# A gather issued one expert earlier, and a routing step moved behind value products, in a fused retention, mixture-of-experts and attention kernel

## The chip, the cores and the metric

The kernel runs on one core of a Trainium2 chip. The metric is the device time of one execution in microseconds (us); lower is better. Engines are named as the profile names them: PE (TensorE; PEld are its weight loads), DVE (VectorE), ACT (ScalarE), POOL (GpSimd) and SP (SyncE, which issues most transfers). Each engine does its instructions in the order in which the program gives them to it.

## The reference

Three layers follow one another, for 2 sequences of 768 tokens, in float32.

```python
# 1. retention: 8 heads of 64, gamma of each head fixed
for t in range(S):
    state = gamma * state + outer(k[:, :, t], v[:, :, t])
    y[:, :, t] = scale * (q[:, :, t] @ state)
x = y as rows of 512

# 2. one expert of 8 for each token; a gate lets a token keep the expert of the token before it
for s in range(S):
    fresh_e = argmax(logits[b, s])                 # logits = x @ w_gate
    e = fresh_e if s == 0 or local_gate[b, s] < 0.5 else prev_e
    prev_e = e
    p = softmax(logits[b, s])
    out[b, s] = p[e] * (relu(x[b, s] @ w1[e]) @ w2[e])     # 512 -> 1024 -> 512

# 3. four causal attention heads of 64; each token takes the two best of them, weighted
for e in range(E2):
    ye = softmax(causal(scale * q_e @ k_e.T)) @ v_e @ wo[e]
    out += weight_of_head(e) * ye
```

## The kernel before, in words

Stage 1 does the retention in six chunks of 128 tokens, for both sequences (0 and 1) in each. For chunk c it has the scores (L307, made at the end of the chunk ahead), which DVE fades with the decay (`fade`, L311, two instructions for each sequence), the products of the past (`outputs_past`, L340), the value products (`outputs_now`, L349, 16 for each sequence), the evacuation of the output by ACT (`evacuate`, L354), and the update of the state (L363, L372). POOL multiplies the decay into keys and queries of the next chunk (`decay_k`, L331; `decay_q`, L325). Q, k and v come in halves of a block, 512 KB each, two chunks ahead.

Between these steps stands the routing of the chunk ahead (class `Route`). `turn_pair` brings the output into rows and the logits beside them (L383, L386). `first` marks the fresh expert (L450 to L461, with a product L453 and its evacuation L458); `held` multiplies the marks `fo` by an identity (PE, L464) and scans along the tokens (DVE, L467), so that a kept token gets the expert of the token before it; `count` scans again (L471) for the place of each token in its expert. Later come `offset`, `rank`, `columns`, `slots`, `marks` (L496), `tokens` (L502, it writes `tt`), `hots` (L507) and `table` (L513), which makes the lists of the tokens of each expert. `shares` (L439, L441) makes the softmax with `nm`, the negated maximum, on DVE and exponentials on ACT. The products L453, L464 and `columns` write parts of one PSUM tile, pR, and `marks` and `tokens` read it. In chunks 4 and 5 some of the first expert's weight pieces are split into a high part `whi` (ACT, L186) and a low part `wlo` (DVE, L191). `busy` (L229) issues dense matmuls on a tile of zeros, whose results nobody reads.

Stage 2 goes over the experts in order of size. Expert e has a hidden half (L873, or L885 and L887) and a value half (`second`, L914 and L918), both on weight pieces that are split five pieces ahead (`prepare`). Its token rows are gathered from x1_d by two indirect DMAs, which POOL issues (`gather`, L220); `gather(e, None)` only reserves the two tiles of a ring of four. `turn2` transposes the gathered rows of expert e + 1 on PE (L809) within the value half of expert e. At the end `put(0)` and `put(1)` scatter the two halves of the result into x2_d, by indirect DMAs that POOL issues too (L940).

Stage 3 does the attention on the rows of x2_d.

In all of stages 1 and 2 the order on every engine is the order of the program text (`manual_schedule`). The order of the parts in a chunk c of stage 1 is:

```python
pYs = [outputs_past(n) for n in ns]
...                                   # columns, slots, first, table, marks, tokens
RT[c - 1].held()                      # PE L464, DVE L467
RT[c - 1].count()                     # DVE L471
RT[c - 2].hots(0, B)                  # DVE L507
for n, pY in zip(ns, pYs):
    outputs_now(n, pY, 0, H // 2)     # PE L349
    evacuate(n, pY)                   # ACT L354
```

Of the kernel before, what the change touches and what calls it, by code (L numbers as in the profile page):

```python
# [21 lines left out]
B, H, S, D = 2, 8, 768, 64  # L22
DM = H * D
C = 128
NC = S // C
# [83 lines left out]
def kernel(  # L109
# [25 lines left out]
    GI = cst.tile([128, 2, E], I32, name="GI")  # L135
# [47 lines left out]
    def split_high(i):  # L183
        hi = ring.tile([128, 1024], F32R, name="whi", bufs=PIECES)
        lo = ring.tile([128, 1024], F32R, name="wlo", bufs=PIECES)
        nc.scalar.activation(hi, raws[i], AF.Copy)  # L186
        pieces[i] = (hi, lo)
# [25 lines left out]
    def gather(e, ix):  # L213
        if e >= E:
            return
        for i in range(2):
            if ix is None:
                XG[e, i] = ring.tile([128, RW], F32, name="xg", bufs=4)
                continue
            nc.gpsimd.indirect_dma_start(  # L220
                out=XG[e, i], out_offset=None, in_=x1_d[:, :],
                in_offset=bass.IndirectOffsetOnAxis(ap=ix[:, i, e:e + 1], axis=0), bounds_check=T, oob_is_err=False)
# [4 lines left out]
    def busy(pw, n, w=4):  # L227
        for _ in range(n):
            nc.tensor.matmul(pw[:, :w * 128], WZ, WZ[:, None, :].to_broadcast([128, w, 128]), start=True, stop=True)  # L229
# [7 lines left out]
    def bank(kind, shape):  # L237
        return psum[-1].tile(shape, F32, name=kind, bufs=2 if kind == "A" else 3)

    with tc.tile_pool(name="s1", bufs=2) as s1:  # L240
        XB, QT, KD, QD, AM, XR, XT, LL = {}, {}, {}, {}, {}, {}, {}, {}
# [8 lines left out]
        def load_pair(c, x):  # L250
            if c >= NC:
                return
            for b in range(B):
                load_half(c * B + b, x)
# [28 lines left out]
        pB = bank("B", [128, 512])  # L283
# [15 lines left out]
        def scores(n, kind):  # L299
            c, b = divmod(n, B)  # L300
            x = XB[n, 0]
            AM[n] = s1.tile([128, 2, H // 2, C], F32, name="am")
            PA[n] = [bank(kind, [128, H // 2, C]) for _ in range(2)]
            for a in range(H // 2):
                for j in range(2):
                    r = slice(j * D, (j + 1) * D)
                    nc.tensor.matmul(PA[n][j][:, a, :], x[r, 1, a * 128:(a + 1) * 128],  # L307
                                     x[r, 0, a * 128:(a + 1) * 128], start=True, stop=True)

        def fade(n, j):  # L310
            nc.vector.tensor_tensor(out=AM[n][:, j], in0=PA[n][j], in1=DT[:, j], op=OP.mult)  # L311
# [15 lines left out]
        def decay_k(n):  # L327
            c, b = divmod(n, B)
            if c < NC - 1:
                KD[n] = s1.tile([128, H, D], F32, name="kd")  # L330
                nc.gpsimd.tensor_tensor(out=KD[n], in0=XB[n, 1][:, 0].rearrange("p (h d) -> p h d", h=H),  # L331
                                        in1=cn("ktab").rearrange("p (c h) -> p c h", c=NC)[:, c, :, None]
                                        .to_broadcast([128, H, D]), op=OP.mult)
# [10 lines left out]
        def outputs_now(n, pY, a0, a1):  # L344
            x = XB[n, 1]
            for a in range(a0, a1):
                for j in range(2):
                    h = 2 * a + j
                    nc.tensor.matmul(pY[j * D:(j + 1) * D, a, :], x[:, 1, h * D:(h + 1) * D], AM[n][:, j, a, :],  # L349
                                     start=n < B, stop=True, skip_group_check=True)  # L350

        def evacuate(n, pY):
            XT[n] = s1.tile([128, H // 2, C], F32, name="xT")
            nc.scalar.activation(XT[n], pY, AF.Copy)  # L354
# [62 lines left out]
        rows, RT = {}, {}  # L417
# [106 lines left out]
        with tc.manual_schedule(engines={ENG.PE, ENG.DVE, ENG.Activation, ENG.Pool, ENG.SP}):  # L524
            for b in range(B):
                decay_k(b)
                scores(b, "AC"[b])
                busy(pB, 3 - b)
                for j in range(2):
                    fade(b, j)  # L530
            nc.gpsimd.tensor_copy(IB, ident)
# [4 lines left out]
            for c in range(NC - 1):  # L536
                load_pair(c + 2, 0)
                if c >= 2:
                    RT[c - 2].offset()
                    RT[c - 2].rank()  # L540
                if c >= NC - 3:
                    fetch_piece(3 * (c - NC + 3))
                if c:
                    part, logits, pv = turn_pair(c - 1)
                    l2 = s1.tile([128, B, E + 1], F32, name="l2")
                    part(0, 8)
                    for b in range(B):
                        logits(b, l2)
                    put_rows(pv)
                    for b in range(B):  # L550
                        send_rows(B * (c - 1) + b)
                if c == 2:
                    nc.sync.dma_start(x1_d[0:1, :], ZR[0:1])
                    for b in range(B):
                        t = b * S + (NC - 1) * C + 1
                        nc.sync.dma_start(x1_d[t:t + C, :], ZR)
                ns = [B * c + b for b in range(B)]
                pYs = [outputs_past(n) for n in ns]
                if c >= 2:
                    RT[c - 2].columns()  # L560
                    RT[c - 2].slots(0, B)
                if c:
                    RT[c - 1] = Route(c - 1)
                    RT[c - 1].first(LL[c - 1], 0, B)
                if c >= 3:
                    RT[c - 3].table(0, B)
                if c >= 2:
                    RT[c - 2].marks(0, B)
                    RT[c - 2].tokens(0, B)
                if c:  # L570
                    RT[c - 1].held()
                    if c == NC - 2:
                        split_high(0)
                    RT[c - 1].count()
                if c >= 2:
                    RT[c - 2].hots(0, B)
                for n, pY in zip(ns, pYs):
                    outputs_now(n, pY, 0, H // 2)
                    evacuate(n, pY)
                    if c == NC - 2 and n == ns[0]:  # L580
                        split_high(1)
                for n in ns:
                    state(n)
                for n in ns:
                    keep(n)
                load_pair(c + 2, 1)
                if c == 1:
                    nc.gpsimd.memset(ZR, 0.0)
                if c >= NC - 3:
                    for i in ((1, 2), (4,))[c - NC + 3]:  # L590
                        fetch_piece(i)
                if c:
                    RT[c - 1].shares(LL[c - 1], 0, B)
                next_qt(c + 2)
                nn = [B * c + 2 + b for b in range(B)]
                if c == NC - 2:
                    split_low(0)
                    split_low(1)
                    nc.gpsimd.tensor_copy(TF[:, :1], pieces[1][1][:, :1].bitcast(F32))
                for f in (decay_k, decay_q)[::1 if c else -1]:  # L600
                    for n in nn:
                        f(n)
                for n in nn:
                    scores(n, "AC"[n % 2])
                    for j in range(2):
                        fade(n, j)
            c = NC - 1
# [19 lines left out]
            V = RT[c - 1] = Route(c - 1)  # L627
# [3 lines left out]
            X.table(0, B)  # L631
            W.marks(0, B)
            W.tokens(0, B)
            V.held()
            V.shares(LL[c - 1], 0, B)
            V.count()
            W.hots(0, B)
            U = Route(c)
            xs = [s1.tile([128, B, DM], F32R, name="blq", bufs=4) for _ in range(2)]
# [34 lines left out]
                                     start=False, stop=m == 1 and b == 1, skip_group_check=True)  # L674

            outputs_now(n0, pYs[0], 0, H // 2)
            evacuate(n0, pYs[0])
            outputs_now(n1, pYs[1], 0, H // 2)
            evacuate(n1, pYs[1])
# [60 lines left out]
            for x in range(2):  # L740
                n = slice(2 * x, 2 * x + 2)
# [55 lines left out]
    with tc.tile_pool(name="mx", bufs=2) as mp:  # L797
# [42 lines left out]
        order = ExitStack()  # L840
        order.enter_context(tc.manual_schedule(engines={ENG.PE, ENG.DVE, ENG.Activation, ENG.Pool, ENG.SP}))
        for e in range(E):
            gather(e + 1, None)
            gather(e + 1, GI)
            if e == 0:
                gather_shares(GS)
            if e == E - 1:
# [9 lines left out]
            def hide():  # L857
                for hi, lo, src in later:
                    nc.scalar.activation(hi, src, AF.Relu)  # L859
                    nc.vector.scalar_tensor_tensor(lo, src, 0.0, hi.bitcast(F32), op0=OP.max, op1=OP.subtract)  # L860
                later.clear()

            for f in range(4):
# [4 lines left out]
                if N > JOIN:  # L868
                    ph = bank("B", [128, 2, CAP])
                    for a in range(2):  # L870
                        n = slice(a * 128, (a + 1) * 128)
# [6 lines left out]
                else:  # L878
                    hc = hh[:, :, 128:] if N <= 192 else None
                    hs.append((hh, hl, hc))  # L880
                    for a in range(2):
                        n = slice(a * 128, (a + 1) * 128)
# [14 lines left out]
                        later.extend(parts)  # L897
                prepare(8 * e + f)
            hide()
            pys = []  # L900
            for i in range(2):
                pys.append(bank("C", [128, DM]))
# [51 lines left out]
            else:  # L954
# [40 lines left out]
                for x in range(2):  # L995
                    n = slice(2 * x, 2 * x + 2)
# [452 lines left out]
```

## Time and profile before

| | |
|---|---|
| time, median of 3 runs | 398.82 us (397.45 to 399.89) |
| the profiled execution: time, span | 398.97 us, 397.2 us |
| stage 1, by the start of its last parts | 0 to about 74 us |
| stage 2 | about 74 to 255 us |
| stage 3 | about 255 to 397 us |
| PE busy | 381.2 us, 96% of the span |
| DVE, ACT, POOL busy | 277.7 us, 237.0 us, 121.2 us |
| mean granted clock of PE | 0.992 |

A row of the timeline has a start, a length, the engine, a line of the kernel, an operation and what it writes and reads, and how many equal instructions were merged into it. In brackets stands how long the engine was idle before it, and what ended that wait. Such a releaser is inferred from semaphores; where an instruction waits for several, the last by the profile is named, and where that one had long been done it was another, often a DMA. Matmuls are pipelined, and their ends are modelled.

### The profile page before, as it was taken

The numbers are of one execution on the slowest core, as the hardware profiler recorded it, in microseconds if no ns is written. First come the engines' busy times: TensorE is split into PE (matmuls) and PEld (weight loads), VectorE is DVE, ScalarE is ACT, GpSimd is POOL, SyncE is SP. The second block draws the span as 40 slices with busy tenths as digits, with TensorE's granted clock in tenths as the row PEclk, the third lists the DMA queues.
The fourth block names the chain that finished last, engine by engine and source line by source line (L and its number), as shares of the span: only waits on it lengthen the run. The fifth ranks groups of instructions, "written<-read, shape, count | busy, mean of one in ns | idle before, by whom it ended". The sixth has DMA issues, their size and how long they took to land.

```text
span 397.2 us, 8425 instructions
## 1 busy us (share of the span) xinstructions
PE 381.2 (96%) x2960; PEld 332.8 (84%) x2960; DVE 277.7 (70%) x785; ACT 237.0 (60%) x547; POOL 121.2 (31%) x175
## 2 busy tenths in 40 slices
PE   8999999999999999989899999999999999999993
PEld 3889996998979797878788698899889988988772
DVE  4556696885676868687787983278986887779630
ACT  1566674283555756677777872267775765668751
POOL 3744432221305012131213020435545332415520
PEclk9999998999999999999999999999999999999998
DMA  7998967477675767777777862131011001001011
GB/s 244 398 358 290 339 234 259 138 252 229 222 248 183 228 231 252 250 227 227 241 242 243 291 235 69 68 115 54 5 50 53 29 2 54 2 27 52 31 54 60
DMA packets 23609, 67.38 MB, mean 170 GB/s; under 512 B 4469, under 2 KB 4725, under 8 KB 23560
## 3 DMA queue, kind: packets, MB, share of 16 engines
q1 hardware_dynamic: 21010, 59.35, 44.7%
q0 software_dynamic: 2544, 7.42, 5.6%
q8 instruction: 25, 0.41, 0.4%
q14 instruction: 24, 0.20, 0.2%
q10 hardware_dynamic: 6, 0.01, 0.0%
HBM read 56.17 MB, written 11.07 MB: 169 GB/s over the span
## 4 chain that ended last, share of the span: by engine, by line
PE 82%; DVE 7%; DMA 5%; ACT 4%; issue 1%; POOL 0%; SPq 0%; POOLq 0%; DVEq 0%; ACTq 0%
PE C L918 18%; PE B L873 8%; PE C L1062 8%; PE C L1238 5%; PE B L1218 5%; PE A L1168 5%; PE C L1257 4%; PE C L1099 4%; DMA xg<-x_d,GI 3%; PE C L349 3%; DVE wlo L191 2%; PE A L307 2%; ACT whi L186 2%; PE A L809 2%; PE A L383 1%; PE B L885 1%
## 5 line engine op out<-in xcount | busy, mean ns | idle before, releaser
L191 DVE TENSOR_TENSOR wlo<-wraw,whi 128x1024 fp32r<-128x1024 f32 x64 | 77.0, 1223 | 16.0 <-ACT whi L186 15.3
L186 ACT ACTIVATE whi<-wraw 128x1024 fp32r<-128x1024 f32 x64 | 65.6, 1049 | 1.3 <-DMA wraw<-in_w_dram 1.2
L940 POOL DMA_INDIRECT x_d<-y,SI x16 | 18.4, 1149 | 136.8 <-ACT y L930 96.0
L1199 POOL TENSOR_SCALAR a<-a,mx,wt 128x128 f32<-128x128 f32 (+5 forms) x48 | 34.2, 721 | 50.4 <-DVE mx L1195 12.8
L918 PE MATMUL C<-whi,hh 128*128 128x512 f32 (+4 forms) x112 | 45.5, 406 | 0.0
L1189 ACT ACTIVATE a<-a,mx 128x128 f32<-128x128 f32 (+5 forms) x48 | 32.0, 668 | 21.5 <-DVE mx L1180 18.3
L918 PE MATMUL C<-whi,hl 128*128 128x512 f32 (+4 forms) x112 | 44.2, 394 | 0.0
L918 PE MATMUL C<-wlo,hh 128*128 128x512 f32 (+4 forms) x112 | 44.1, 394 | 0.0
L885 PE MATMUL B<-xx,whi 128*128 128x384 f32 (+3 forms) x100 | 30.9, 363 | 0.0
L1180 DVE CUSTOM_DVE_ANT_0 a<-A,MR 128x384 f32<-128x384 f32 (+3 forms) x48 | 25.3, 530 | 2.4 <-PE A L1168 2.0
L1218 PE MATMUL B<-K,a 128*128 128x128 f32 x168 | 26.3, 274 | 0.0
L887 PE MATMUL B<-xx,wlo 128*128 128x192 f32 (+3 forms) x100 | 25.7, 257 | 0.0
L918 PEld LDWEIGHTS C<-whi,hl 128*128 128x128 f32 (+4 forms) x112 | 20.0, 179 | 5.9
L918 PEld LDWEIGHTS C<-wlo,hh 128*128 128x128 f32 (+4 forms) x112 | 20.1, 180 | 4.9
L918 PEld LDWEIGHTS C<-whi,hh 128*128 128x128 f32 (+4 forms) x112 | 20.1, 179 | 4.5
L859 ACT ACTIVATE hh<-t 128x128 fp32r<-128x128 f32 (+4 forms) x56 | 16.3, 318 | 12.1 <-DVE t L891 9.9
L1218 PEld LDWEIGHTS B<-K,a 128*128 128x128 f32 x168 | 19.8, 140 | 2.4 <-issue 0.7
L1168 PE MATMUL A<-ks,qh 128*128 128x256 f32 (+3 forms) x56 | 21.6, 385 | 0.1
L1238 PE MATMUL C<-at,vv 128*64 128x256 f32 (+1 forms) x192 | 21.5, 359 | 0.0
L220 POOL DMA_INDIRECT xg<-x_d,GI x14 | 15.6, 1116 | 13.2 <-DVE z L763 9.2
L1238 PEld LDWEIGHTS C<-at,vv 128*64 128x64 f32 x192 | 13.4, 136 | 7.2 <-issue 1.4
L885 PEld LDWEIGHTS B<-xx,whi 128*128 128x128 f32 x100 | 18.8, 188 | 0.6
(321 smaller groups left out, 980.6 us busy)
## 6 DMA issues: line engine op xcount, KB each, us to landing
wraw<-in_w_dram SPq DMA_DIRECT2D x64, 512.0 KB, 4.2
blq<-in_blk_dram SPq DMA_DIRECT2D x12, 512.0 KB, 7.9
blk<-in_blk_dram SPq DMA_DIRECT2D x12, 512.0 KB, 6.6
x_d<-xr SPq DMA_DIRECT2D x12, 260.0 KB, 7.5
out_dram<-y SPq DMA_DIRECT2D x12, 256.0 KB, 2.0
xr<-x_d SPq DMA_DIRECT2D x10, 256.0 KB, 2.6
x_d<-ZR SPq DMA_DIRECT2D x2, 260.0 KB, 5.9
wraw<-in_wv_dram SPq DMA_DIRECT2D x1, 520.0 KB
```

Source lines behind the costliest of these rows:

```text
L186: nc.scalar.activation(hi, raws[i], AF.Copy)
L191: nc.vector.tensor_tensor(out=lo, in0=raws.pop(i), in1=hi.bitcast(F32), op=OP.subtract)
L873: nc.tensor.matmul(ph[:, a, :N], w[:, k, n], x[:, k, :N], start=m == 0, stop=m == 11)
L885: nc.tensor.matmul(pa[:, :, :N], wh[:, k, n], XX[e][:, k, :, :N], start=k == 0, stop=False, skip_group_check=True)
L887: nc.tensor.matmul(pa[:, 1, :N], wl[:, k, n], XX[e][:, k, 0, :N], start=False, stop=k == 3, skip_group_check=True)
L918: nc.tensor.matmul(pys[i][:rows], h[:, a, n], w[:, a, :], start=f == 0 and a == 0 and m == 0, stop=f == 3 and a == 1 and m == 2)
L1062: nc.tensor.matmul(pp, w[:, k, a * 128:(a + 1) * 128], x[:, k, :], start=m == 0, stop=m == 11)
L1168: nc.tensor.matmul(ps[:, :w], qq[b, g, e][:, tq], KS[b, e][:, s0:s0 + w], start=m == 0, stop=m == 1)
L1189: nc.scalar.activation(AA[u][:, :n], AA[u][:, :n], AF.Exp, bias=mx[:, 0, i:i + 1], scale=-1.0, accum_out=mx[:, 1, i:i + 1])
L1199: nc.gpsimd.tensor_scalar(a[:, :n], a[:, :n], mx[:, 1, i:i + 1], WT[b, g][:, i, e:e + 1], op0=OP.mult, op1=OP.mult)
L1218: nc.tensor.transpose(pT[:, s - s0, :], a[:, s * C:(s + 1) * C], ident)
L1238: nc.tensor.matmul(po[j * HD:(j + 1) * HD, c0:], VV[b, s][:, e * HD:(e + 1) * HD], at[j][:, s, c0:], start=s == 0, stop=s == ns - 1, skip_ ...
```

## The change

Three things change, in order of place.

First, the dense matmuls between the scores of chunk 0 become fewer: 1 instead of 3 behind the scores of sequence 0, none instead of 2 behind those of sequence 1.

Second, `held` and `count` of the chunk ahead move, in each of the chunks 1 to 5, from before the value products to behind those of the first sequence and before their evacuation. In chunk 5 `shares` moves with them. In chunk 4 the split of weight piece 0 on ACT, which stands between the two, goes along.

Third, in stage 2 the gather for expert e + 2 is issued between the hidden half and the value half of expert e, from e = 1 on. The gathers for experts 1 and 2 stay at the start of experts 0 and 1. Until now the gather for e + 1 was issued at the start of e.

```diff
@@ -525,7 +525,7 @@
                 scores(b, "AC"[b])
-                busy(pB, 3 - b)
+                busy(pB, 1 - b)
                 for j in range(2):
                     fade(b, j)
@@ -567,15 +567,15 @@
                     RT[c - 2].marks(0, B)
                     RT[c - 2].tokens(0, B)
-                if c:
-                    RT[c - 1].held()
-                    if c == NC - 2:
-                        split_high(0)
-                    RT[c - 1].count()
                 if c >= 2:
                     RT[c - 2].hots(0, B)
                 for n, pY in zip(ns, pYs):
                     outputs_now(n, pY, 0, H // 2)
+                    if c and n == ns[0]:
+                        RT[c - 1].held()
+                        if c == NC - 2:
+                            split_high(0)
+                        RT[c - 1].count()
                     evacuate(n, pY)
                     if c == NC - 2 and n == ns[0]:
                         split_high(1)
@@ -631,9 +631,6 @@
             W.marks(0, B)
             W.tokens(0, B)
-            V.held()
-            V.shares(LL[c - 1], 0, B)
-            V.count()
             W.hots(0, B)
@@ -674,6 +671,9 @@
             outputs_now(n0, pYs[0], 0, H // 2)
+            V.held()
+            V.shares(LL[c - 1], 0, B)
+            V.count()
             evacuate(n0, pYs[0])
             outputs_now(n1, pYs[1], 0, H // 2)
             evacuate(n1, pYs[1])
@@ -840,8 +840,9 @@
         for e in range(E):
-            gather(e + 1, None)
-            gather(e + 1, GI)
+            if e < 2:
+                gather(e + 1, None)
+                gather(e + 1, GI)
             if e == 0:
                 gather_shares(GS)
@@ -897,6 +898,9 @@
                 prepare(8 * e + f)
             hide()
+            if e:
+                gather(e + 2, None)
+                gather(e + 2, GI)
             pys = []
```

## Rows read from the trace of the kernel before

**Rows 1.** The page: span, and busy time of PE (share, instructions).

```profile
span 397.2 us, 8425 instructions
...
PE 381.2 (96%) x2960; PEld 332.8 (84%) x2960; DVE 277.7 (70%) x785; ACT 237.0 (60%) x547; POOL 121.2 (31%) x175
```

**Rows 2.** Waits of PE, 0 to 75 us: for whom, us, times, longest.

```profile
PE B L464 <- DVE tt L502: 2.3, 4, 0.7
...
PE B L464 <- DVE fo L461: 0.7, 1, 0.7
```

**Rows 3.** Waits of PE, 75 to 260 us.

```profile
PE A L809 <- DMA xg<-x_d,GI: 3.1, 3, 1.5
PE A L809 <- DVE hh L860: 1.2, 1, 1.2
```

**Rows 4.** Timeline around expert 3: start, length, instruction, idle before and releaser.

```profile
141.58 1.03 POOL L940 DMA_INDIRECT x_d<-y,SI  x1 [12.44 <-ACT y L930]
...
148.41 0.93 POOL L940 DMA_INDIRECT x_d<-y,SI  x1 [5.79 <-DVE hl L860]
149.65 1.40 POOL L220 DMA_INDIRECT xg<-x_d,GI  x1 [0.30 <-issue]
...
154.91 0.63 PE L809 MATMUL A<-K,xg 128*128 128x128 f32 x4 [0.55 <-DMA xg<-x_d,GI]
```

**Rows 5.** Timeline of PE, the first transposes within expert 5.

```profile
197.58 0.63 PE L809 MATMUL A<-K,xg 128*128 128x128 f32 x4 [1.25 <-DVE hh L860]
```

**Rows 6.** Timeline of PE, the held product of chunk 2.

```profile
30.32 0.23 PE L464 MATMUL B<-IB,fo 128*128 128x128 bf16 x1 [0.68 <-DVE tt L502]
```

**Rows 7.** Timeline of chunk 0: scores, dense matmuls, fades, value products.

```profile
6.67 1.93 PE L307 MATMUL A<-blq 64*128 64x128 f32 x16 [0.16 <-DMA blq<-in_blk_dram]
...
8.52 0.82 PE L229 MATMUL B<-WZ 128*128 128x512 bf16 x3
8.62 1.29 DVE L311 TENSOR_TENSOR am<-A,DT 128x512 f32<-128x512 f32 x2 [2.16 <-PE A L307]
...
9.28 1.16 PE L307 MATMUL C<-blq 64*128 64x128 f32 x16
...
10.37 0.60 PE L229 MATMUL B<-WZ 128*128 128x512 bf16 x2
...
10.90 1.99 PE L349 MATMUL C<-am,blk 128*64 128x128 f32 x32
```

**Rows 8.** Timeline of chunk 1: POOL's decays, DVE's first comparison, value products.

```profile
14.80 2.52 POOL L325 TENSOR_TENSOR qd<-blq,qt 128x512 f32<-128x512 f32 x2 [1.91 <-DMA qt<-in_qtab_dram]
...
17.28 2.04 POOL L331 TENSOR_TENSOR kd<-blk,K 128x512 f32<-128x512 f32 x2
...
18.41 0.94 DVE L450 TENSOR_TENSOR eq<-L,K 128x16 bf16<-128x16 f32 x1
...
20.55 1.97 PE L349 MATMUL C<-am,blk 128*64 128x128 f32 x32
```

**Rows 9.** Windows: stretch, length, busy PE, PEld, DVE, ACT, POOL, granted clock, DMA, GB/s.

```profile
20.50:30.40 9.90, 9.22 (x136) 8.83 (x135) 5.74 (x19) 5.99 (x18) 4.51 (x4) 1.00 0.99 345
50.30:60.40 10.10, 9.44 (x144) 9.07 (x143) 9.36 (x24) 7.04 (x17) 3.96 (x5) 1.00 0.58 219
206.00:228.70 22.70, 21.22 (x120) 17.64 (x119) 18.53 (x34) 17.49 (x31) 4.56 (x4) 1.00 0.79 263
```

**Rows 10.** Timeline of chunks 4 and 5: first fades, tokens, `nm`, first evacuation.

```profile
54.36 1.29 DVE L311 TENSOR_TENSOR am<-A,DT 128x512 f32<-128x512 f32 x2
...
60.02 0.18 DVE L502 TENSOR_TENSOR tt<-B,K 128x32 bf16<-128x32 f32 x1
...
60.93 0.14 DVE L439 TENSOR_SCALAR nm<-mx 128x2 f32<-128x2 f32 x1
...
61.69 0.57 ACT L354 ACTIVATE xT<-C 128x512 f32<-128x512 f32 x1
```

**Rows 11.** Windows of half a us, the tail of stage 1, with the granted clock.

```profile
66.50:67.00 0.50, 0.50 (x3) 0.23 (x2) 0.47 (x2) 0.50 (x2) 0.25 (x1) 0.50 0.12 49
```

## Prediction

> **What bounds the kernel now.** I read the page first, then the busy time by stretch, then the waits of TensorE (PE), then the timeline around each wait. The page says that PE is busy 381.2 us of the 397.2 us of the span [rows 1]. So the kernel is bound by PE, and whatever a reordering can win lies in the 16 us in which PE stands still. The waits of PE name two places that the diff touches. In stage 1 the held product (L464) waits five times, 0.7 + 2.3 = 3.0 us in all, for VectorE (DVE) to finish `fo` or `tt` [rows 2]. PE works in order, so the 32 value products of the chunk (L349), which need neither, stand behind it. In stage 2 the transposes of the next expert's rows (L809) wait four times, 3.1 us by name for the gathered rows and 1.2 us by name for DVE [rows 3]. These are the prices on offer, 7.3 us; the question is how much of each arrives at the end.
>
> **The gather, place and price.** Look at expert 3 in the order of GpSimd (POOL) [rows 4]. The first scatter of the expert ahead is issued at 141.58. The second is issued only at 148.41, 6.8 us later. The view names a DVE instruction for this wait, but both scatters write x2_d, and 6.8 us is what one needs to land: I read it as the landing of the first scatter. The gather comes behind the second scatter in POOL's order and is issued at 149.65. PE gets to the transposes and waits 0.55 us, until 154.91, 5.3 us after the issue. The gather is thus late because POOL's queue holds it behind two scatters that follow one another.
>
> The edit puts the gather for expert e + 2 between the hidden half and the value half of expert e. On POOL nothing but the gathers stands between the second scatter of e - 1 and the first scatter of e, and a gather waits for no result of the hidden half. So it will be issued where today's gather for e + 1 is issued, just behind the second scatter of e - 1; what changes is that these rows are wanted one whole expert later. Its buffer is free: the ring has four, and the rows of expert e, which lie in the same two, were transposed in the value half of e - 1. Each gather is two DMAs on POOL's queue, as before, and their number is the same; only during expert 1 are there four in a row (for 2, then for 3). The two for 2 are first, so nothing that is wanted soon stands behind the new ones. POOL's next work, the first scatter of e, has to wait for the whole value half anyway.
>
> I count the fourth wait (197.58, 1.25 us [rows 5], put down to DVE `hh`) as a gather's too: the products of the value half ahead of it in PE's queue have used those `hh` already. Price: 3.1 + 1.2 = 4.3 us. If that fourth wait were DVE's own, 3.1. What cover takes over? Behind the transposes PE needs the weight pieces; nothing in the waits of stage 2 is put down to them today [rows 3], so I take no new wait, and keep the weights as a rival.
>
> **Held product and count, chunks 1 to 3.** The edit moves L464 behind the first 16 value products, 0.9 us by the starts of L349. `tt` is ready by then in chunk 2, where L464 stood idle 0.68 us [rows 6], and the scan behind it on DVE comes 0.3 us later than today while `hots` is done in its place: no loss there, since DVE next waits for scores. Chunk 2 gives 0.68; the other three waits on `tt` share 2.3 - 0.68 = 1.6, some 0.54 each, so chunk 3 gives 0.54. Together 1.2 us.
>
> Chunk 1 is different, and the warm-up is part of it. The edit takes four of the five dense matmuls (L229) out of chunk 0. They lie on PE's path: three take 0.82 us, and the second scores follow them [rows 7]. With one left, the second scores begin 0.55 earlier, at 8.75, and end at 9.9. The first pair of fades also ends at 9.91 (8.62 + 1.29), so the first value products start there. The second fades then run from 9.95 to 11.25; today's second value products start at about 11.8 (10.90 + 0.9). So chunk 0 gains about 0.5 us, not 4 x 0.27 = 1.1. Of this, little passes through chunk 1. There DVE's first comparison (L450) takes 0.94 us and ends at 19.35, just as POOL's pair of decay products ends (17.28 + 2.04 = 19.32) [rows 8]. That pair follows the `qd` pair, which began at 14.80, when the DMA of `qt` landed. A transfer's landing does not move with PE. I take L450's end as fixed at 19.35; a product with its result stands ahead of the value products, so these start at about 19.5 instead of 20.55: 1.05 us from chunks 0 and 1 together. Were L450 simply long, it would move along and the sum would be 0.5 + 0.7 = 1.2; the bounds lie close.
>
> The Trainium skill (GPSIMD Engine Reference, section Specifications) says that POOL shares its SBUF interfaces with DVE and contends with DVE instructions that read two SBUF inputs. L450 is such an instruction, and by that rule its end stays with POOL's: 1.05, not 1.2.
>
> **Chunks 4 and 5.** Here DVE is the engine to watch: it is busy 9.36 of 10.1 us [rows 9]. In chunk 4 it has the split of two weight pieces between `count` and the fades, and runs without a pause to the fades at 54.36 [rows 10]. Reordering saves it only the 0.1 us by which its wait for L464 gets shorter (0.33 today, some 0.2 behind `hots`). The same holds in chunk 5, where `tt` ends at 60.2 behind a third split. And there `shares` moves as well: its `nm` (60.93) releases two exponentials on ScalarE (ACT) that stand ahead of the evacuation of the first output (61.69) in ACT's order, after the edit as now. `nm` comes behind `hots` and the scan, which is 0.1 earlier at best. So of the 1.1 us of PE waits in these two chunks I take 0.15 us; the bounds are 0 and 1.1. The rest of stage 1 (60 to 74) is a chain of short steps and moves along.
>
> **Sum.** Stage 1: 1.05 + 1.2 + 0.15 = 2.4. Stage 2: 4.3. Together 6.7 us. Stage 3 is not touched. The profiled execution took 398.97 us (span 397.2), 0.15 above the median of 398.82, so the two need no correction: 398.97 - 6.7 = 392.3 us.
>
> **Rivals.**
> A, the forecast, 392.3. Its own range comes from the bounds: the fourth wait DVE's own (1.2 less) to chunks 4 and 5 given whole (0.95 more) and chunk 1 at 1.2: 391.1 to 393.5.
>
> B, the transfers hold stage 1. In its chunks the DMA engines are busy 0.99 of the time [rows 9], and a shorter chunk wants the same bytes sooner. Against it: PE waits for a chunk's load only at the very start (the first scores), and the loads are two chunks ahead. If nothing of stage 1 comes, 398.97 - 4.3 = 394.7.
>
> C, the weights take the place of the gather. In expert 6 the DMA engines are at 0.79, and DVE is busy 18.5 of 22.7 us [rows 9]; take the stall away and DVE is at 18.5 of 21.2. A value product would then wait for `wlo`. Against it: splits run five pieces ahead, and no wait of PE is put down to them. Half of stage 2's gain lost gives 394.5, all of it 396.6; I take 395.5.
>
> D, slower: the clock. By its durations PE began at its lower level: the 16 products of the first scores started over 1.85 us (6.67 to 8.52), those of the next over 1.09 (9.28 to 10.37), 1.7 times as fast [rows 7]. The four dense matmuls came just behind that rise, and in a sparse stretch of the tail the granted clock does fall, to 0.50, the 1.2 GHz level [rows 11]. If the clock fell back after the edit, each us of full-speed work would take 0.7 us more. 6.7 / 0.7 = 9.6 us of such work use up the whole gain, 15 us make the kernel over 1% slower; two chunks (18 us of PE work) would give 392.3 + 12.6 = 405. Against it: the clock had already risen before the matmuls that go, and the later chunks, which hold no dense matmul and stood idle at the held product, kept 1.00 [rows 9].
> The Trainium skill (TensorE: Matmul & The Clock Gate, Part 1) says that the throttled clock is the default and that activity releases it. By that rule fewer warm-up matmuls can only hurt; that is D. The rows agree that PE starts low.
>
> That the edit of the gather does nothing, because POOL waits in between, is no rival of weight: its index and buffers are ready.
>
> **How the numbers follow.** A 0.63, B 0.14, C 0.15, D 0.04; 0.04 is left for what I do not see. The likeliest gives 392.3. The range reaches below A for runs that lie as far from the median as those of before (397.45 to 399.89) and above to B and most of C: 390.6 to 395.2. One per cent, about what a measurement of this kernel tells from no change, is 4.0 us, so faster means below 394.8. A lies there, B at its edge (half), C by a third: 0.63 + 0.07 + 0.05, and 0.02 of the unseen: 0.77. D and a little of the unseen are slower: 0.05. The rest, 0.18, is the same.
>
> **What would show it.** Right: no wait of L464 in chunks 2 and 3, none of L809; the gather for e + 2 issued just behind the second scatter of e - 1; L450 of chunk 1 still ending at about 19.35; `nm` of chunk 5 later behind its `tt` than today. Wrong: idle time of L349, L307 or the decay products put down to a load (B); of L918 to `wlo` (C); 16 scores over 1.8 us after the first ones (D); L809 still waiting at expert 5 (the fourth wait was DVE's).

## The result, and the profile after

| | before | changed kernel |
|---|---|---|
| time, median of 11 runs | 399.32 us (397.45 to 400.49) | 394.23 us (391.96 to 397.19) |
| ratio to before | | 0.9886, 95% interval 0.9853 to 0.9918 |
| the profiled execution: time, span | 398.97, 397.2 us | 394.20, 392.4 us |
| PE busy | 381.2 us | 381.4 us |

The kernel became faster by 1.1%, 4.6 us by the ratio; the forecast was 6.7 us and 392.3. The span of the profiled execution became 4.8 us shorter, all of it idle time of PE. These are the waits of PE in the changed kernel, up to 72 us and from 72 to 256 us; they answer to [rows 2] and [rows 3].

```profile
PE B L229 <- DVE WZ L231: 1.0, 1, 1.0
PE A L645 <- ACT xT L354: 0.6, 1, 0.6
PE B L874 <- ACT x0h L725: 0.2, 1, 0.2
...
PE B L963 <- DMA xg<-x_d: 1.4, 1, 1.4
PE B L874 <- ACT x0h L725: 0.2, 1, 0.2
```

No wait of the held product (L464) and none of the transposes (L809) is left. Three waits are new: 0.6 us before the gate products in the tail of stage 1 (L645, L648 before), 0.2 us in the first products of stage 2 (L874, L873 before; it lies at 72 us and so stands in both answers), and 1.4 us before the first rows within expert 7 (L963, L959 before). The starts of PE's parts, read from both timelines, show where the time came from and where it went:

| stretch of PE, from and to the start of | before | after | difference |
|---|---|---|---|
| span's start, first scores | 6.67 | 6.44 | -0.23 |
| first scores, value products of chunk 1 | 13.88 | 12.82 | -1.06 |
| chunk 1 to chunk 2 | 9.93 | 9.33 | -0.60 |
| chunk 2 to chunk 3 | 9.93 | 9.52 | -0.41 |
| chunks 3 to 5 | 20.01 | 19.03 | -0.98 |
| chunk 5, stage 2 | 13.20 | 14.17 | +0.97 |
| stage 2, value half of expert 7 | 166.29 | 161.68 | -4.61 |
| value half of expert 7, first rows | 5.58 | 7.16 | +1.58 |
| first rows, end of the span | 151.71 | 152.25 | +0.54 |

The differences add up to -4.8. At the value half of expert 7 the changed kernel was 6.9 us ahead.

**The gather.** The timeline around expert 3 (compare [rows 4]):

```profile
146.21 1.05 POOL L944 DMA_INDIRECT x_d<-y,SI  x1 [5.50 <-DVE t L892]
147.56 1.58 POOL L220 DMA_INDIRECT xg<-x_d,GI  x1 [0.30 <-PE B L888]
...
152.29 0.60 PE L809 MATMUL A<-K,xg 128*128 128x128 f32 x4
```

The gather (now of expert 5) is issued right behind the second scatter, as before. The transposes at 152.29 (of expert 4's rows, gathered an expert earlier) have no idle time ahead of them.

**The new wait within expert 7.** Timeline of the changed kernel from the last splits of expert 6 to the first rows:

```profile
221.67 1.06 ACT L186 ACTIVATE whi<-wraw 128x1024 fp32r<-128x1024 f32 x1 [1.32 <-DMA wraw<-in_w_dram]
...
223.30 1.06 ACT L186 ACTIVATE whi<-wraw 128x1024 fp32r<-128x1024 f32 x1 [0.57 <-DMA wraw<-in_w_dram]
...
224.78 1.06 ACT L186 ACTIVATE whi<-wraw 128x1024 fp32r<-128x1024 f32 x1 [0.42 <-DMA wraw<-in_w_dram]
...
225.75 0.67 ACT L934 ACTIVATE y<-C,pc 128x512 f32<-128x512 f32 x1
...
226.69 1.27 POOL L944 DMA_INDIRECT x_d<-y,SI  x1 [18.01 <-ACT y L934]
...
232.01 3.52 POOL L944 DMA_INDIRECT x_d<-y,SI  x1 [4.04 <-DVE hl L876]
...
234.62 0.68 DVE L876 SCALAR_TENSOR_TENSOR hl<-B,hh 128x512 fp32r<-128x512 f32 x1
...
237.39 0.80 SPq L853 DMA_DIRECT2D xg<-x_d  x2
...
240.15 1.24 PE L963 MATMUL B<-K,xg 128*128 128x128 f32 x8 [1.42 <-DMA xg<-x_d]
```

And the same steps before:

```profile
229.08 1.06 ACT L186 ACTIVATE whi<-wraw 128x1024 fp32r<-128x1024 f32 x1 [0.47 <-DMA wraw<-in_w_dram]
...
230.05 0.67 ACT L930 ACTIVATE y<-C,pc 128x512 f32<-128x512 f32 x1
230.99 1.33 POOL L940 DMA_INDIRECT x_d<-y,SI  x1 [13.24 <-ACT y L930]
...
236.69 1.44 POOL L940 DMA_INDIRECT x_d<-y,SI  x1 [4.37 <-DVE hl L875]
...
240.14 0.80 SPq L852 DMA_DIRECT2D xg<-x_d  x2
...
245.49 1.03 PE L959 MATMUL B<-K,xg 128*128 128x128 f32 x8
```

Read these rows against the start of expert 7's hidden half (228.51 before, 221.59 after). PE reached the first rows 17.0 us behind it before, and would have after. ACT stands 2.3 us on weight pieces that have not landed (1.2 us before): its last split came 4.3 us earlier than before (229.08, 224.78), for a PE that was 6.9 us ahead. The evacuation stands behind that split and came 1.5 us behind the start of the hidden half before and 4.2 us after. Its result goes into the first scatter, the second scatter waits for the first one (it began 8.2 us behind that start before, 10.4 us after), and the load of the first rows waits for both.

This lateness is only half of it. The second scatter also took 3.52 us on POOL instead of 1.44; it lies beside DVE instructions that follow one another without a pause, and it ended 0.23 us behind the last of them (`hl` at 234.62). So the load was issued 15.8 us behind that start instead of 11.6. Before, by an estimate with the 2.76 us from the load's issue to the first rows after (237.39 to 240.15), it had 2.6 us to spare. The lateness of the second scatter (2.2 us) or its length (2.1 us) alone would have fitted into that; the two together did not.

### The profile page after: what moved, and what is told of

Its sections match the earlier page's. It is cut to its first block, busy times and chain, and to the rows that moved or that the text cites. A ratio compares the mean times of both kernels' runs of the same rounds, so it can differ in the third digit from the quotient of the medians.

```text
span 392.4 us, 8418 instructions
## 1 busy us (share of the span) xinstructions
PE 381.4 (97%) x2956; PEld 333.8 (85%) x2956; DVE 275.5 (70%) x785; ACT 235.5 (60%) x547; POOL 124.9 (32%) x175
## 4 chain that ended last, share of the span: by engine, by line
PE 75%; DVE 10%; ACT 8%; issue 3%; DMA 3%; ACTq 0%; SPq 0%; DVEq 0%
PE C L922 13%; PE C L1066 7%; PE B L874 6%; ACT whi L186 5%; PE C L1242 5%; PE B L1222 5%; PE C L1261 4%; PE A L1172 4%; PE C L1103 4%; DVE wlo L191 4%; PE C L349 3%; PE B L886 2%; PE C L340 2%; PE B L229 2%; PE A L307 2%
## 5 line engine op out<-in xcount | busy, mean ns | idle before, releaser
L944 POOL DMA_INDIRECT x_d<-y,SI x16 | 21.1, 1318 | 128.0 <-ACT y L934 86.2
## 6 DMA issues: line engine op xcount, KB each, us to landing
blk<-in_blk_dram SPq DMA_DIRECT2D x12, 512.0 KB, 10.2
```

## The experiments

The kernels e1 to e12 stand below in the order e1, e2, e3, e4, e5, e10, e6, e7, e12, e9, e8, e11.

**Each part alone.** Four kernels hold one part or two. In the first only the gather moved:

```diff
 # before, with
+            if e < 2:
-            gather(e + 1, None); gather(e + 1, GI)
+                gather(e + 1, None); gather(e + 1, GI)
...
             hide()
+            if e:
+                gather(e + 2, None); gather(e + 2, GI)
```

> Of the change only the gather for expert e + 2 in the middle of expert e; stage 1 is that of the kernel before. The forecast's sum: the four waits of L809 go, 4.3 us, and nothing takes their place: about 395.0 (before at 399.3). Rival, from the profile of the changed kernel: with stage 2 shorter the last weight pieces come late, ScalarE waits for them with the evacuation of expert 6's first half behind it, and so the scatter and the load of the first rows (L959) come late: PE waits there for 1 to 1.5 us, and the gain is about 3 us, 396.3. The wait of L959 on the load tells the two apart.

Measured: 394.61 us, ratio 0.9881 (0.985 to 0.9911). The gather alone brings as much as the whole change. From stage 2's start to expert 7's value half its profile has 161.27 us against 166.29, 5.0 us less. Then comes the rival's wait:

```profile
PE B L963 <- DMA xg<-x_d: 2.4, 1, 2.4
```

So both are right in part. The forecast's time (395.0) was met by the median, and the gain of stage 2 is larger than forecast, but a loss stands behind it. In the profiled execution (395.14) the two together leave 2.4 us, not 4.3. The rest of its 3.8 us of shorter span comes mainly from stretches that this edit does not touch: the first scores begin 0.6 us earlier, the stretch from them to chunk 1 is 0.3 us shorter, and that from chunk 5 to stage 2 is 0.5 us shorter.

In the second only `held`, `count` and `shares` moved:

```diff
 # before, with
-                if c:
-                    RT[c - 1].held()
...
                     outputs_now(n, pY, 0, H // 2)
+                    if c and n == ns[0]:
+                        RT[c - 1].held()
...
-            V.held(); V.shares(LL[c - 1], 0, B); V.count()
...
             outputs_now(n0, pYs[0], 0, H // 2)
+            V.held(); V.shares(LL[c - 1], 0, B); V.count()
```

> Of the change only held, count and shares behind the first value products; all five dense matmuls stay and the gathers stay where they were. Forecast: chunk 1 gives its wait, 0.7 us, chunks 2 and 3 together 1.2, chunks 4 and 5 with the tail 0.15: 2.0 us, about 397.3. If shares did not stand ahead of the evacuation the last two chunks would give another 1.0: 396.3.

Measured: 397.40 us, ratio 0.9964 (0.9938 to 0.9991): 1.4 us, with 2.0 (a ratio of 0.995) inside the interval and 3.0 outside. No wait of L464 is left in its profile, and the 0.6 us before the gate products is there.

In the third only the warm-up shrank:

```diff
-                busy(pB, 3 - b)
+                busy(pB, 1 - b)
```

> Of the change only one dense matmul instead of five in chunk 0. Forecast's step: chunk 0 gains 0.5 us; L450 of chunk 1 ends at 19.35 as now, tied to GpSimd, PE waits for it, and 0.1 to 0.4 us arrive at the end: about 399.0. Rival: L450 moves along, and 0.5 us arrive. Rival (clock): with fewer dense matmuls the granted clock stays at 1.2 GHz for longer, at the start or in the tail of stage 1, in some executions: mean granted clock under 0.990 and 1 to 3 us longer.

Measured: 398.44 us, ratio 0.9987 (0.9968 to 1.0006). L450 of chunk 1 did not end at 19.35 in its profile but at 18.78, and PE did not wait for it. The time lies between no change and 1.3 us; 0.1 to 0.4 fits, and the full 1.1 us cannot be told apart from it by this alone. Ten of its 12 executions had a mean granted clock of 0.995 or more: the fewer dense matmuls did not keep the clock low.

The fourth is the changed kernel with the line above put back.

> The changed kernel with all five dense matmuls back in chunk 0. By the forecast 0.3 to 0.6 us slower than the changed kernel: 394.5 to 394.8. Rival (clock): the executions of the changed kernel differ by 5 us and those with a mean granted clock of 0.988 are the longer ones; if the missing matmuls cause that, these executions stay at 0.993 and about 393, as fast as the changed kernel or faster.

Measured: 393.80 us, ratio 0.9881 (0.9846 to 0.9915), the same as the changed kernel; the 0.3 to 0.6 us of the expectation are too small to be seen here. Two of its six executions had a mean clock of 0.988 and took 396.4 and 396.8, so the missing matmuls are not what makes such executions. Its profile is one of them. The windows of one us around the first rows (columns as in [rows 9]):

```profile
240.00:241.00 1.00, 0.00 (x0) 0.00 (x0) 0.66 (x2) 0.30 (x1) 0.00 (x0) 1.00 0.88 303
241.00:242.00 1.00, 0.62 (x5) 0.50 (x6) 0.21 (x1) 0.69 (x1) 0.00 (x0) 0.96 0.37 139
242.00:243.00 1.00, 1.00 (x6) 1.00 (x6) 0.00 (x0) 0.00 (x0) 0.33 (x1) 0.50 0.00 0
243.00:244.00 1.00, 1.00 (x4) 0.81 (x3) 0.00 (x0) 0.00 (x0) 0.69 (x1) 0.50 0.00 0
244.00:245.00 1.00, 1.00 (x4) 0.71 (x4) 0.00 (x0) 0.00 (x0) 0.00 (x0) 0.50 0.69 262
245.00:246.00 1.00, 1.00 (x5) 0.83 (x4) 0.00 (x0) 0.00 (x0) 0.00 (x0) 0.83 0.00 0
246.00:247.00 1.00, 1.00 (x6) 0.79 (x5) 0.00 (x0) 0.00 (x0) 0.00 (x0) 1.00 0.00 0
```

PE stands 2.0 us in front of the first rows, and then the granted clock is 0.50, the 1.2 GHz level, for over 3 us of dense work. From the first rows to stage 3 this execution took 10.83 us instead of 9.09: the wait is paid a second time, with 1.7 us.

**The wait within expert 7.** Evacuation and scatters of expert 6 go ahead of the last splits:

```diff
                     second(f, 1)
+                    if e == E - 2 and f == 3:
+                        put(0)
+                        put(1)
                     prepare(8 * e + 4 + f)
...
-                put(0)
-                put(1)
+                if e < E - 2:
+                    put(0)
+                    put(1)
```

> The changed kernel, in which expert 6 evacuates and scatters its result before the last weight splits of its value half, not behind them. Theory: these splits wait on ScalarE for late weight pieces, the evacuation stands behind them, and by way of the two scatters that follow one another the load of the first rows (L959's) is late. Then the scatter starts some 3 us earlier against expert 7's hidden half, PE's wait of 1.6 to 2.6 us before the first rows goes, and with it the second stretch at 1.2 GHz that some executions show just behind it: about 392.0 (changed kernel 394.2), and no execution with a mean granted clock under 0.990. Rival: the load is late because of the scatters themselves (their time to land, or GpSimd's 3.5 us for one of them beside VectorE's splits): the wait stays at 1 us or more, 394.

Measured: 392.34 us, ratio 0.9838 (0.9801 to 0.9875), all six executions at 0.990 or more. The interval overlaps that of the changed kernel (0.9853 to 0.9918), so the verdict rests on the timeline:

```profile
222.50 0.67 ACT L934 ACTIVATE y<-C,pc 128x512 f32<-128x512 f32 x1
...
223.44 1.48 POOL L944 DMA_INDIRECT x_d<-y,SI  x1 [14.48 <-ACT y L934]
...
231.72 0.96 POOL L944 DMA_INDIRECT x_d<-y,SI  x1 [6.79 <-DVE hl L876]
...
235.26 0.80 SPq L853 DMA_DIRECT2D xg<-x_d  x2
...
238.53 1.03 PE L967 MATMUL B<-K,xg 128*128 128x128 f32 x8
```

The evacuation is 0.95 us behind the start of the hidden half, the load is issued 2.1 us earlier than in the changed kernel, and PE does not wait. But the theory's path is not what the rows show. The first scatter starts 3.2 us earlier against the hidden half, yet 8.3 us pass from it to the second instead of 5.3, and the second begins 10.2 us behind the start of the hidden half, where it began at 10.4. What became shorter is the second scatter itself, 0.96 us instead of 3.52: the rival's term.

All kept profiles say the same. The second scatter took 3.35 to 4.04 us in the four in which PE waits for the first rows (the changed kernel, e1, e4 and e8), and at most 1.96 us in the other ten. One of these, e6 below, has the evacuation as late as the changed kernel, 4.2 us behind the start of the hidden half (222.38), and no wait:

```profile
233.56 1.02 POOL L944 DMA_INDIRECT x_d<-y,SI  x1 [4.79 <-DMA x_d<-y,SI]
...
239.36 1.08 PE L963 MATMUL B<-K,xg 128*128 128x128 f32 x8
```

That the edit helps, the executions show: of the 27 of the five kernels that have it (e5, e7, e9, e11, e12) none has a mean granted clock under 0.990, of the 29 of the changed kernel, e4, e6 and e8 13 have. Why the second scatter is long in one order and short in the other is not shown.

A second way to take ACT's wait away is to ask for the pieces later:

```diff
-            if slot >= NP - 12:
-                n += min(PIECES - AHEAD, slot - NP + 13)
+            if slot >= NP - 8:
+                n += min(PIECES - AHEAD, slot - NP + 9)
```

> The changed kernel, in which the splits of weights run five pieces ahead until the end of expert 6, and the catching up (up to ten ahead) begins with expert 7 instead of in the value half of expert 6. Theory: it is the catching up that asks for pieces which the transfers have not brought yet; without it ScalarE does not wait on pieces in expert 6's value half, the evacuation and scatter come some 3 us earlier, the wait before the first rows (L959's) goes: about 392.2, as e5. Rival: the transfers are late whatever is asked of them, and PE then waits for pieces in expert 7: 394 or more.

Measured: 398.11 us, ratio 0.9964 (0.9941 to 0.9987), far from the 392.2 of the theory. Its first half held: the evacuation came at 221.14, and the wait before the first rows went. But the waits around expert 7 show a larger one:

```profile
ACT wkh L793 <- DMA wraw<-in_wk_dram: 9.0, 1, 9.0
...
PE C L922 <- ACT hh L875: 5.2, 1, 5.2
```

SP issues the transfers in order. Now the load of stage 3's weights (`wk`) stands behind the load of the first rows, which waits for the scatters: it is issued at 235.22 instead of 222.97. ACT waits 9.0 us for it with an evacuation behind it, and PE stands 5.2 us. The catching up is what brings these transfers ahead of that wait.

**Shares of chunk 5.** Only its place changes:

```diff
             V.held()
-            V.shares(LL[c - 1], 0, B)
             V.count()
             evacuate(n0, pYs[0])
             outputs_now(n1, pYs[1], 0, H // 2)
             evacuate(n1, pYs[1])
+            V.shares(LL[c - 1], 0, B)
```

> The changed kernel with shares of chunk 5 behind both evacuations instead of ahead of the first. Theory: the two exponentials ahead of the first evacuation cost PE its wait of 0.6 us before the gate products; without them the wait goes and the tail of stage 1 is 0.6 to 0.7 us shorter: 393.6. Rival: the evacuation waits for the products alone, or the gate products then wait for the count: no difference.

Measured: 393.13 us, ratio 0.9863 (0.9816 to 0.991). The wait before the gate products is gone from its profile; by the medians 1.1 us, by the intervals not told apart from the changed kernel. The profile itself shows no gain in stage 1: 0.3 us of idle time before the held product of chunk 5 take the place of that wait, and from chunk 4 to stage 2 it takes 23.8 us, the changed kernel 23.7. Together with the scatter it is clearer:

> The changed kernel with both edits, the scatter of expert 6 before its last weight splits and shares behind the evacuations. Both theories right and independent: 391.4. If the earlier end of stage 1 only brings stage 2's weights under more pressure: as the first edit alone, 392.0.

Measured: 390.73 us (390.18 to 391.76), ratio 0.9798 (0.9763 to 0.9832). This interval lies below that of the changed kernel: it has the shortest median here and is 2.0% faster than before. From chunk 5 to stage 2 it takes 13.54 us, the kernel with the scatter alone 14.37. With the five dense matmuls of chunk 0 put back into it:

> The kernel of e7 (changed, scatter of expert 6 first, shares of chunk 5 later) with all five dense matmuls back in chunk 0. By the forecast's step for the warm-up 0.3 to 0.6 us slower than e7's 390.7: 391.2. Rival: the four matmuls lie on PE's path in full, 1.1 us: 391.8. Rival: they change nothing because the loads of chunk 1 set the start: 390.7.

Measured: 391.50 us, ratio 0.9796 (0.9761 to 0.9832). By the ratios no difference, by the medians 0.8 us. The intervals have room for nothing as for the full 1.1 us, so the forecast's 0.3 to 0.6 is neither shown nor refuted.

**The place of the move in chunk 5.** In the kernel with the scatter first, only chunk 5 goes back to the order of before:

```diff
             W.tokens(0, B)
+            V.held(); V.shares(LL[c - 1], 0, B); V.count()
             W.hots(0, B)
...
             outputs_now(n0, pYs[0], 0, H // 2)
-            V.held(); V.shares(LL[c - 1], 0, B); V.count()
```

> The kernel of e5 (changed, with expert 6's scatter before its last weight splits), in which chunk 5 has held, shares and count back ahead of the value products; chunks 1 to 4 stay changed. By the forecast the move in chunk 5 is worth next to nothing, as PE's wait of 0.66 us before the held product only turns into its wait of 0.6 before the gate products: within 0.2 us of e5's 392.3, with the first wait back and the second gone. Rival: the move in chunk 5 is worth its 0.6 us: 392.9. Second question, the granted clock: if the idle time before the gate products makes the clock fall in the tail, most executions go back to a mean of 0.997 and gain 0.4 to 0.7: 391.8.

Measured: 392.55 us, ratio 0.9839 (0.9802 to 0.9876), against 392.34 and 0.9838 with the move. The wait before the held product is back and that before the gate products is gone:

```profile
57.78 0.23 PE L464 MATMUL B<-IB,fo 128*128 128x128 bf16 x1 [0.77 <-DVE tt L502]
...
58.44 0.14 DVE L439 TENSOR_SCALAR nm<-mx 128x2 f32<-128x2 f32 x1
...
59.21 0.57 ACT L354 ACTIVATE xT<-C 128x512 f32<-128x512 f32 x1
...
59.90 1.04 PE L648 MATMUL A<-IW,xT 128*128 128x9 f32 x8
```

The move in chunk 5 is worth nothing, as the sum had it; and with chunk 5 as before, chunks 3 to 5 take 20.04 us, before 20.01, so chunk 4 gives nothing by itself either. Its second question was answered no: the clock still fell in the tail.

**The clock in the tail of stage 1.** Two dense matmuls fill the wait before the gate products:

```diff
             V.offset()
+            busy(warm, 2)
             gate(0)
```

> The changed kernel with two dense matmuls on zeros ahead of the first gate products, where PE waits 0.6 us. Theory: moving the held product moved PE's idle time into the sparse tail of stage 1, and that is why the granted clock falls to 1.2 GHz there in nearly every execution with the move and in few without; with the dense matmuls it stays up, mean granted clock 0.997 instead of 0.993 where the end of stage 2 is undisturbed, and the time is 0.4 to 0.7 us shorter. Rival: the sparse products behind them decide, the clock falls as before, and the time is the same or up to 0.2 us longer.

Measured: 395.50 us, ratio 0.9882 (0.9829 to 0.9934); no execution above 0.993. The granted clock falls in the tail as before. The theory that PE's idle time there makes it fall is refuted twice, by this kernel and by the one before.

**The place of the gather.** In the kernel with the scatter first, the gather for e + 2 stands at the start of expert e:

```diff
+            if e:
+                gather(e + 2, None); gather(e + 2, GI)
             if e == 0:
...
             hide()
-            if e:
-                gather(e + 2, None); gather(e + 2, GI)
```

> The kernel of e5, in which the gather for expert e + 2 stands at the start of expert e, where the gather for e + 1 stood, instead of at its middle. By the forecast GpSimd gets to it at the same moment in both, behind the second scatter of expert e - 1: same time as e5, 392.3 within 0.5. Rival: the place in the middle matters, because the gather's transfers collide with something at the start: 1 us or more slower.

Measured: 392.03 us, ratio 0.9811 (0.9776 to 0.9847), no slower than the middle (392.34, 0.9838). The timeline of POOL around expert 3:

```profile
146.15 0.94 POOL L944 DMA_INDIRECT x_d<-y,SI  x1 [6.11 <-DVE hl L864]
147.39 1.08 POOL L220 DMA_INDIRECT xg<-x_d,GI  x1 [0.30 <-issue]
```

As in the changed kernel, the gather follows the second scatter. That it is for an expert later matters; its line in the middle does not.

## Why the prediction was right, point by point

The measured time, 394.23, lies in the range (390.6 to 395.2), 1.9 us above the likeliest, and on the forecast side. The mechanisms that the sum names for the gather and the held product held. The step on what takes over behind the gather failed, and the price of chunks 0 and 1 came out by another path.

- **The gather, 4.3 us: right in kind, a little small.** All four waits of L809 went, the one by name DVE's among them. The stretch shortened by 5.0 us (161.27 in the kernel with the gather alone). The four waits summed to 4.3 us of idle time; each stretch lost about 0.2 us more than the idle time ahead of its transposes, as 1.58 us were lost at the first rows for 1.42 us of idle time. In the profiled execution 0.4 us of it are hidden: the products of expert 0's hidden half took 11.81 us instead of 11.41. Some kernels' profiles have the one, some the other, and what decides it is open.
- **No new wait behind it: wrong.** The step "What cover takes over?" looked only at the transposes' own successors and took no new wait. The cover that ran out was that of the first rows in expert 7: PE came to them 17.0 us behind the start of its hidden half, and the load was there in time by some 2.6 us. Rival C had one half of the cause, late weight pieces, but the wrong victim: not a value product that waits for `wlo`, but an evacuation on ACT behind the splits and, by way of two scatters and a load, PE itself. The other half, a second scatter that took 3.52 us on POOL instead of 1.44, stands in no rival. The price was 1.58 us in the profile, 2.2 to 2.6 in the kernels e4 and e1, and 1.7 more where the clock fell behind it. Five of the 11 executions of the changed kernel had a mean clock of 0.987 or 0.988 and took 395.3 to 397.2 us; the other six took 392.0 to 394.2. Their traces were not taken; that they are executions with this second stretch rests on e4's and e8's profiles, which have the same mean and show it.
- **Stage 1, 2.4 us: right in sum.** 2.3 in the profile by the table, of which 0.2 lie before the first scores and so ahead of every edit. Chunks 0 and 1: -1.06 for 1.05. Chunks 2 and 3: -1.01 for 1.2. Chunks 4, 5 and the tail: -0.98 + 0.97, nothing, for 0.15.
- **L450: tied to POOL, but not fixed in time, and not what PE waits for.** The rows that answer to [rows 8]:

```profile
16.44 2.23 POOL L331 TENSOR_TENSOR kd<-blk,K 128x512 f32<-128x512 f32 x2
...
17.33 1.95 PE L340 MATMUL C<-qd,SB 128*128 128x128 f32 x16
...
18.01 0.69 DVE L450 TENSOR_TENSOR eq<-L,K 128x16 bf16<-128x16 f32 x1
...
19.11 0.22 PE L453 MATMUL B<-IB,eq 128*128 128x128 bf16 x1
```

 It ends at 18.70, as POOL's pair does at 18.67. But POOL's decay products began at 13.99 instead of 14.80: the landing of `qt` moves from execution to execution. In the profile of e1 it ends with the first of the two instructions of that pair (17.66 and 17.63), not with the pair. The rule of the Trainium skill (GPSIMD Engine Reference, section Specifications), that DVE instructions with two SBUF inputs contend with POOL for its SBUF interfaces, agrees with both profiles; what it could not say is when POOL begins. PE, however, did not wait for L450: the product with its result (L453) follows the products of the past (L340) without idle time, 1.78 us behind their start, after as before. The 1.06 us are made up otherwise: 0.17 of chunk 0, for which 0.5 was taken, and 0.89 of the held product's place, 0.67 of it PE's wait. That they come to the forecast's 1.05 is luck.
- **The tail of stage 1: right.** `nm` follows `tt` by 1.10 us (57.73 to 58.83) instead of 0.91 [rows 10], and stands ahead of the evacuation:

```profile
58.83 0.15 DVE L439 TENSOR_SCALAR nm<-mx 128x2 f32<-128x2 f32 x1
...
59.59 1.06 ACT L354 ACTIVATE xT<-C 128x512 f32<-128x512 f32 x2
...
60.22 1.06 PE L645 MATMUL A<-IW,xT 128*128 128x9 f32 x8 [0.61 <-ACT xT L354]
```

- **Rival B (transfers hold stage 1)** did not come: no PE wait for a chunk's load in the changed kernel. Its wait exists, though: in the profiles of e7 and e11 the first value products of chunk 0 wait 0.5 and 0.8 us for `blk`.
- **Rival D (the clock)** did not come at its place: behind the warm-up the granted clock stayed at 1.00. But the clock cost time elsewhere, at a wait that the sum did not have. The Trainium skill (TensorE: Matmul & The Clock Gate, Part 1) has a PE that has idled fall back to the throttled clock. Here a fall stands behind a wait of 2.0 us (e4) and none behind one of 2.4 us (e1), so the length of the wait alone does not decide, and what does is open.

## What to carry to other kernels

When a stall that sits in several places of a pipelined loop goes, ask what else was paced by it: here the stalls gave the weight transfers the time they needed, and the lateness came out in another place, where an engine did the urgent evacuation behind splits that could wait. There 2.6 us were to spare, and it took a second delay, the long scatter, to use them up; so ask, of each transfer that is in time today, by how much. Put what the end waits for ahead of what is only prefetched, on every queue that it passes, and price a moved step on the queue it is really held by: the line of the program says little where the queue is in order. A wait that only changes its place (chunk 5) can be seen from the next engine's order before it is tried.

## What the runs showed of the hardware that was not expected

In the tail of stage 1 the granted clock falls to 0.50 for 3 to 4 us in the profiles of all eleven kernels in which the held product moved; of the other three it does so before, and not in those with the gather or the warm-up alone. The mean granted clock, a rough sign of it, says the same of the executions: 6 of 80 of the former have 0.995 or more, 48 of 68 of the latter. In the profiles it costs 0.5 to 0.8 us: from chunk 5 to stage 2 13.20 us before, with the fall, and 12.70 and 12.36 in the kernels with the gather or the warm-up alone, without it. Neither the idle time in the tail (e8) nor the order in chunk 5 (e9) decides it; what does is open.

From stage 2 to the start of stage 3, an indirect DMA took between 0.92 and 2.10 us on POOL, with a median of about 1.04. The exception is one in each of four profiles, the second scatter of expert 6, with 3.35 to 4.04 us. In all four it ended 0.23 or 0.24 us behind the last of a run of DVE instructions without a pause.
